# An attention and mixture-of-experts kernel: another opening, a later load of values, and half of a copy moved to VectorE in three steps

## The chip, the cores and the metric

The kernel runs on one core of one Trainium2 chip. The metric is the device time of one execution in microseconds (us). The engines are called as in the profile: PE is TensorE (PEld its weight loads), DVE is VectorE, ACT is ScalarE, POOL is GpSimd, SP is SyncE, which here only issues transfers. A time such as "at 8.08" is counted from the start of the profiled span.

## The reference

Attention over 4 batches, 8 heads, 768 positions and head dimension 64, with a window of 128 positions and 4 sink positions that all rows see; its output, as 3072 rows of 512, goes through a two-level top-1 mixture of experts (4 groups of 4 experts, hidden width 1024):

```python
scores = scale * np.matmul(q, k.transpose(0, 1, 3, 2))
is_sink = pos[None, :] < int(n_sink)
rel = pos[:, None] - pos[None, :]
in_window = (rel >= 0) & (rel < int(window))
scores = np.where(is_sink | in_window, scores, -1e9)
a = np.exp(scores - scores.max(-1, keepdims=True))
attn = np.matmul(a / (a.sum(-1, keepdims=True) + 1e-9), v)
...
g_idx = np.argmax(x @ w_group, axis=1)          # then the expert of the group in the same way
h = np.maximum(xg @ w1[g, e], 0.0)
out[tok_idx] = g_w * e_w * (h @ w2[g, e])
```

`n_sink` and `window` are inputs, so the masks are made on the chip from two 64-bit integers.

## The kernel before

**Tiling.** The 3072 rows are worked in 24 attention steps of 128 queries (6 per batch). The two halves of 64 queries of a step are folded onto 128 partitions, so that a head's scores are 128x136: 4 sink columns, 128 of the window, 4 more. The MoE follows in parts, and fills gaps of the later attention steps.

**One step.** In step i the code works on four ages of data: scores of i, transposes of a = i-1, values of b = i-2, and the router's logits of c = i-3. On PE, in the written order: `scores(i, 0)` and `scores(i, 1)` (four heads each, into two tiles `ps`, 32 products in all), `trans(a)` (16 transposes of the probabilities `pt` into `tp`), some products on zeros (`warm`, 8, 10 and 6 of them in steps 0 to 2, from the list `FILL`), `values(b, 0)`, `logits(c)`, `sink_t(a)` (two transposes of the sink probabilities `sp` into columns 256 to 319 of the same `tp`), `natural(c)` (transposes of the result), `values(b, 1)`. Where an age does not exist yet (steps 0 to 2) its part is missing.

On DVE: `maxima(i, g)` for the two halves g: one `COPY_PREDICATED` that folds the window's parts in `ps` (not in the first step of a batch), then for each of the four heads a masked copy `sm<-ps,msk` with the row's maximum. Then `norm(c)`, which scales the result (`xt<-tp,rc`), and in step 3 `tables()`, small tables for routing (`colm`, `trib` and others). On ACT: `evac(a, 0)` and `evac(a, 1)` copy the transposed probabilities of four heads each from `tp` in PSUM to `pa` in SBUF (two `COPY pa<-tp`); then the 8 exponentials of step i (`pt<-sm,st`), between them `sink_evac` (`spT`), and the copy of a result (`xT`). On POOL: for each half two selects (`pu<-pa`, `pa<-pa`) that split `pa`'s triangle, copies of the sink rows into `pu`, and the packing of `sp`.

**Buffers that tie them.** `sink_t(a)` writes columns of `tp` that the second half of `evac(a, ..)` reads (columns 256 to 511), so it waits for that copy. `scores(i+1)` writes the `ps` that `maxima(i)` reads. `values(b, 0)` and `(b, 1)` need `pa`, `pu` and the values `vv`.

**Order.** Each engine executes its instructions in the order in which the code records them; a wait of one holds all that stand behind it on that engine. The same holds for SP and its transfers. All instructions of these helpers carry line 118 in the profile, since one function records them.

**The opening.** POOL writes two integer tables (row minus column, and column). DVE casts them to `diff` and `col`, cuts `dq` out of `diff`, and makes the masks `msk`. The scalars come by a transfer `ni`, are cast to `nf` and spread to all partitions by one product with ones (`lg<-nf,colm`); DVE copies the result and rebuilds the two 64-bit numbers from their words in three instructions (`lneg` twice, `sv`; `sv` holds the sink count and the window), and a fourth makes `wd`. Before and after the product PE runs 14 and 6 products on zeros. `load_s(0)` and `load_v(0)`, the values of step 0, are issued ahead of the loop.

Of the kernel before, what the change touches and what calls it, by code (L numbers as in the profile page):

```python
# [22 lines left out]
P = 128  # L23
# [22 lines left out]
NEG = -1.0e30  # L46
# [101 lines left out]
def moe_attention(tc, kqT, vN, vS, nsw, wgx, wgd, w1, w2, out):  # L148
    nc = Pinned(tc)
    v = nc.vector  # L150
    with ExitStack() as top, ExitStack() as att:
# [17 lines left out]
        def const(shape, dt, name):  # L169
            return cp.tile(shape, dt, name=name)  # L170
# [10 lines left out]
        qb = wk.tile([P, NQ, HP, P], F32, name="qb", bufs=1)  # L181
        xx = un[:, 0:NDC * W].rearrange("p (c w) -> p c w", w=W)
        hx = un[:, NDC * W:(NDC + NFC) * W].rearrange("p (f w) -> p f w", w=W)
        dif = gp.tile([P, P], I32, name="xg")
        nc.gpsimd.iota(dif, pattern=[[-1, P]], base=0, channel_multiplier=1)
        coli = gp.tile([P, P], I32, name="xg")
        nc.gpsimd.iota(coli, pattern=[[1, P]], base=0, channel_multiplier=0)
        act = const([P, 1], F32, "act")
        nc.gpsimd.memset(act, 0.0)
        nc.gpsimd.memset(colm[0:1], 1.0)  # L190
        nc.gpsimd.memset(kb[:, :, 0:BW], 0.0)
        vts, env, bat = {}, {}, {}

# [71 lines left out]

        route_reset(tab)

        diff = const([P, P], F32, "diff")
        v.tensor_copy(diff, dif)
        col = const([P, P], F32, "col")  # L270
        v.tensor_copy(col, coli)
        dq = gp.tile([P, D], F32, name="xg")
        for r in (0, D):
            v.tensor_copy(dq[r:r + D], diff[r:r + D, r:r + D])
        isu = gp.tile([P, D], F32, name="xg")
        v.tensor_scalar(isu, dq, 0.0, None, ALU.is_lt)
        rel = gp.tile([P, D], F32, name="xg")
        v.scalar_tensor_tensor(rel, isu, float(P), dq, ALU.mult, ALU.add)
        nf1 = const([1, 4], F32, "nf1")
        v.tensor_copy(nf1, ni)  # L280
        warm(WARM)
        nc.tensor.matmul(ob[0][:, 0:4], colm[0:1], nf1, start=True, stop=True)
        warm(WARM2)
        msk = const([P, 3, SW], F32, "msk")
        mb, ms, mc = msk[:, :, 0:D], msk[:, :, D:D + 2 * NSK], msk[:, :, D + 2 * NSK:]
        v.tensor_scalar(mb[0:D, 0], dq[0:D], 0.0, NEG, ALU.mult, ALU.add)
        v.tensor_scalar(ms[:, 0, 0:NSK], col[:, 0:NSK], 0.0, NEG, ALU.is_ge, ALU.mult)
        wd = const([P, 1], F32, "wd")
        nf = const([P, 4], F32, "nf")
        v.tensor_copy(nf, ob[0][:, 0:4])  # L290
        lneg = const([P, 2], F32, "lneg")
        v.tensor_scalar(lneg, nf[:, 0::2], 0.0, 4294967296.0, ALU.is_lt, ALU.mult)
        v.tensor_tensor(lneg, lneg, nf[:, 0::2], ALU.add)
        sv = const([P, 2], F32, "sv")
        v.scalar_tensor_tensor(sv, nf[:, 1::2], 4294967296.0, lneg, ALU.mult, ALU.add)
        nsk, win = sv[:, 0:1], sv[:, 1:2]
        v.tensor_scalar(wd, win, -float(D), None, ALU.add)
        snk = gp.tile([P, D], F32, name="xg")
        v.tensor_scalar(mc[:, 2], rel, win, NEG, ALU.is_ge, ALU.mult)
        v.tensor_scalar(snk, col[:, 0:D], nsk, NEG, ALU.is_lt, ALU.mult)  # L300
        v.tensor_scalar(mb[:, 2], dq, wd, NEG, ALU.is_ge, ALU.mult)
        v.scalar_tensor_tensor(mc[:, 0], isu, NEG, mc[:, 2], ALU.mult, ALU.add)
        v.tensor_tensor(mb[D:P, 0], mb[D:P, 2], snk[D:P], ALU.add)
        v.tensor_scalar(ms[:, 0, NSK:], col[:, 0:NSK], nsk, NEG, ALU.is_ge, ALU.mult)
        v.tensor_tensor(mc[0:D, 0], mc[0:D, 0], snk[0:D], ALU.add)
        selu = const([P, D], I32, "selu")
        val = const([P, NI], F32, "val")

        def other_masks():
            v.tensor_scalar(selu, dq, 0.0, None, ALU.is_lt)  # L310
            v.tensor_copy(ms[:, 2], ms[:, 0])
            v.tensor_copy(msk[:, 1], msk[:, 2])
            v.tensor_tensor(snk[0:D], snk[0:D], isu[0:D], ALU.mult)
            v.tensor_tensor(mc[0:D, 1], mc[0:D, 1], snk[0:D], ALU.add)
# [19 lines left out]

        def tables():
            v.tensor_scalar(colm, col, -float(P), None, ALU.add)
            v.tensor_scalar(trib, diff, 0.0, None, ALU.is_lt)
            v.tensor_scalar(rev, col[:, 0:4], -1.0, 4.0, ALU.mult, ALU.add)
            v.tensor_scalar(edge, col[:, 0:MAXT + 1], float(P), None, ALU.mult)
            v.tensor_copy(val, prti)  # L340
            v.tensor_scalar(gen[:, 0:1], win, 1.0, None, ALU.is_lt)
            v.tensor_scalar(gen[:, 1:2], win, float(P), None, ALU.is_gt)
            v.tensor_scalar(gen[:, 2:3], nsk, float(NSK), None, ALU.is_gt)
            v.tensor_reduce(gen[:, 3:4], gen[:, 0:3], AX.X, ALU.max)
# [460 lines left out]
                    r = slice(f * D, (f + 1) * D)  # L805
                    nc.tensor.transpose(env["tp"][:, f, h * D:(h + 1) * D], e["pt"][r, h, NSK:NSK + P], ident[r, r])

        def evac(i, g):
            e = env[i]
            pa = wk.tile([P, 4, P], F32, name="pa", bufs=4)  # L810
            nc.scalar.copy(pa.rearrange("p h (f q) -> p f h q", f=2),
                           env["tp"][:, :, 4 * g * D:4 * (g + 1) * D].rearrange("p f (h q) -> p f h q", q=D))
            e["pT", g] = [pa, pu[i % 2][g]]
            if i % NT:
                for dst, sg in ((pu[i % 2][g], -1), (pa, 1)):
                    nc.gpsimd.affine_select(out=dst[0:D], in_=pa[0:D], pattern=[[0, 8], [sg, D]], compare_op=ALU.is_ge,
                                            fill=0.0, base=(sg - 1) // 2, channel_multiplier=-sg)
# [390 lines left out]

        ew = early_work(PARTS[0][0])
        room_v(-1)  # L1210
        load_s(0)
        load_v(0)
        rest = None
        for i in range(NI):
            a, b, c = i - 1, i - 2, i - 3
            mid, far, old = a >= 0, b >= 0, c >= 0
            state["clk"] += 3.0
            scores(i, 0)
            scores(i, 1)
            if i + DEPTH < NI:  # L1220
                load_q(i + DEPTH)
            if mid:
                env["tp"] = pair()
                trans(a)
                evac(a, 0)
                evac(a, 1)
            warm(FILL[i] if i < len(FILL) else 0, ob[0][:, 224:416])
            if far:
                values(b, 0)
                load_s(b + 1)  # L1230
            if i + DEPTH < NI:
                load_k(i + DEPTH)
            if i == 0:
                load_v(1)
            if old:
                logits(c)
            if mid:
                sink_t(a)
            if old:
                natural(c)  # L1240
            maxima(i, 0)
            exps(i, 0)
            maxima(i, 1)
            if i == NI - 1:
                sink_evac(a)
            if old:
                norm(c)
            routing(1, ("pe",))
            exps(i, 1, (0, 1))
            if mid and i < NI - 1:  # L1250
                sink_evac(a)
            exps(i, 1, (2, 3))
            if mid:
                sink_rows(a)
            if i < NI - 1:
# [396 lines left out]
```

## Time and profile before

| | us |
|---|---|
| median of 3 runs | 489.07 (487.38 to 489.42) |
| the profiled execution | 484.39 |
| its span, first to last instruction | 482.7 |
| outside the span | 1.69 |

The page of the profile gives, for each engine, its busy time over the span, and the chain of work that ended last, followed back from the last instruction. The timeline of one engine lists its instructions in order, neighbours of a kind in one row; a bracket gives the idle time ahead of a row and what released it. Spans of PE's rows overlap by about 0.07 us, since the ends of pipelined products are modelled. The name of a releaser is that of the semaphore event that came last, which need not be the one that mattered.

### The profile page before, as it was taken

How to read it: one execution, taken by the hardware profiler on the slowest of the kernel's cores; microseconds unless marked ns; L12 is line 12 of the kernel's file. 1: busy time of each engine (PE TensorE's matmuls, PEld its weight loads, DVE VectorE, ACT ScalarE, POOL GpSimd, SP SyncE). 2: the span in 40 equal slices, each digit the busy share in tenths (PEclk: the TensorE clock that was granted, in tenths of full speed). 3: DMA queues.
4: the chain of work that ended last, by engine and by line, in shares of the span. 5: the costliest groups of instructions: out<-in, count | busy, mean ns of one | idle time of the engine just before them, and what ended most of it. 6: DMA issues, size and time to landing. Idle time of an engine off the chain costs nothing.

```text
span 482.7 us, 14712 instructions
## 1 busy us (share of the span) xinstructions
PE 465.3 (96%) x5429; PEld 390.0 (81%) x5429; DVE 374.7 (78%) x1181; ACT 330.2 (68%) x858; POOL 168.4 (35%) x267
## 2 busy tenths in 40 slices
PE   7999999999989999999999999999999999999994
PEld 6788878888779888887989789569876977977974
DVE  7576888899989989987714876488687997999750
ACT  5999989899893445766615765278446786788741
POOL 3674765664662122221203124033302713103102
PEclk9999999999999999999999999999999999999998
DMA  8698878989978937934952358596949983999300
GB/s 260 177 286 277 275 250 245 272 258 318 289 233 274 336 103 245 311 135 150 377 217 85 110 176 299 197 330 267 311 169 372 411 314 111 362 405 337 108 22 30
DMA packets 58836, 117.09 MB, mean 243 GB/s; under 512 B 8574, under 2 KB 20990, under 8 KB 58754
## 3 DMA queue, kind: packets, MB, share of 16 engines
q1 hardware_dynamic: 54162, 102.65, 62.5%
q0 software_dynamic: 4320, 13.26, 7.8%
q8 instruction: 45, 0.74, 0.6%
q14 instruction: 37, 0.30, 0.2%
q10 hardware_dynamic: 272, 0.15, 0.1%
HBM read 103.25 MB, written 13.03 MB: 241 GB/s over the span
## 4 chain that ended last, share of the span: by engine, by line
PE 67%; DVE 17%; ACT 7%; issue 4%; POOL 3%; DMA 1%; POOLq 0%; DVEq 0%; SPq 0%; ACTq 0%
PE ph L118 30%; PE po L118 28%; PE tp L118 5%; ACT pt L118 3%; DVE sm L118 3%; DVE wlo L118 3%; PE ps L118 3%; DVE xt L118 2%; POOL pu L118 2%; ACT whi L118 1%; PE lg L118 1%; DVE ps L118 1%; ACT pa L118 1%; DVE lt L118 1%; DVE un L118 1%
## 5 line engine op out<-in xcount | busy, mean ns | idle before, releaser
L118 DVE TENSOR_TENSOR wlo<-rw,whi 128x1024 fp32r<-128x1024 f32 x112 | 135.0, 1223 | 24.9 <-ACT whi L118 23.5
L118 PE MATMUL ph<-un,whi 128*128 128x256 f32 (+9 forms) x576 | 128.0, 312 | 0.3
L118 PE MATMUL po<-whi,un 128*128 128x512 f32 (+5 forms) x384 | 127.8, 396 | 0.0
L118 ACT CAST whi<-rw 128x1024 fp32r<-128x1024 f32 (+1 forms) x115 | 115.6, 1025 | 10.5 <-DMA rw<-in_w 5.6
L118 POOL DMA_INDIRECT out<-ot,sidx x32 | 43.2, 1351 | 227.7 <-ACT ot L118 129.3
L118 PE MATMUL ph<-un,wlo 128*128 128x256 f32 (+10 forms) x416 | 99.1, 263 | 0.0
L118 PEld LDWEIGHTS ph<-un,whi 128*128 128x128 f32 x576 | 93.7, 189 | 2.2 <-DVE un L118 0.8
L118 PEld LDWEIGHTS po<-whi,un 128*128 128x128 f32 (+4 forms) x384 | 70.4, 185 | 25.1 <-issue 6.7
L118 ACT ACTIVATE pt<-sm,st 128x136 f32<-128x136 f32 x192 | 76.1, 402 | 7.4 <-DVE st L118 5.3
L118 PE MATMUL po<-wlo,un 128*128 128x512 f32 (+6 forms) x200 | 77.5, 389 | 0.0
L118 PEld LDWEIGHTS ph<-un,wlo 128*128 128x128 f32 x416 | 76.7, 189 | 0.6
L118 DVE CUSTOM_DVE_ANT_0 sm<-ps,msk 128x136 f32<-128x136 f32 x192 | 45.8, 296 | 7.3 <-PE ps L118 1.1
L118 PEld LDWEIGHTS po<-wlo,un 128*128 128x128 f32 (+5 forms) x200 | 36.0, 180 | 7.6
L118 POOL DMA_INDIRECT xg<-xd,gidx x30 | 33.1, 1104 | 24.2 <-DMA rw<-in_w 11.6
L118 PE MATMUL ps<-kb,qb 64*64 64x208 f32 (+1 forms) x768 | 38.4, 333 | 2.0 <-DVE st L118 1.4
L118 DVE TENSOR_TENSOR hc<-ph,hc 128x160 f32<-128x160 f32 (+6 forms) x64 | 21.3, 338 | 21.6 <-ACT hc L118 21.4
L118 POOL COPY pu<-spT 32x512 f32<-32x512 f32 x46 | 28.6, 649 | 26.3 <-ACT spT L118 25.4
L118 ACT ACTIVATION_READ_ACCUMULATOR pt<-sm,st 128x1 f32 x192 | 36.8, 192 | 0.0
L118 ACT ACTIVATE ot<-po,cg 128x512 f32<-128x512 f32 (+6 forms) x25 | 17.0, 681 | 28.1 <-PE po L118 28.1
L118 PEld LDWEIGHTS ps<-kb,qb 64*64 64x64 f32 x768 | 26.5, 132 | 7.3 <-DVE st L118 2.1
L118 POOL TENSOR_SCALAR_AFFINE_SELECT pu<-pa 64x512 f32<-64x512 f32 x40 | 26.4, 660 | 15.7 <-ACT pa L118 15.7
L118 ACT COPY hc<-ph 128x160 f32<-128x160 f32 (+6 forms) x64 | 19.4, 304 | 17.8 <-PE ph L118 17.0
(204 smaller groups left out, 717.6 us busy)
## 6 DMA issues: line engine op xcount, KB each, us to landing
rw<-in_w SPq DMA_DIRECT2D x128, 512.0 KB, 5.9
vv<-in_vN SPq DMA_DIRECT2D x24, 512.0 KB, 5.2
kb<-in_kqT SPq DMA_DIRECT2D x23, 288.0 KB, 3.9
qb<-in_kqT SPq DMA_DIRECT2D x24, 256.0 KB, 4.6
xd<-xt SPq DMA_DIRECT2D x24, 256.0 KB, 3.7
vv<-in_vS SPq DMA_DIRECT2D x24, 128.0 KB, 3.5
out<-ot,sidx POOLq DMA_INDIRECT x32, 4.9
xg<-xd,gidx POOLq DMA_INDIRECT x30, 4.9
```

Source lines behind the costliest of these rows:

```text
L118: r = f(*a, **k)
```

## The change

It has three parts.

1. **Opening.** POOL's IOTA writes `dq` (two blocks of 64x64) and `col` directly as f32; the casts and cuts on DVE are gone, and the table `diff` is made by a further IOTA in `tables()`, in step 3. The two scalars are combined on PE: `nf1` gets two more columns (is the low word negative), and three products with one row of ones or of 4294967296.0 add up in two columns of `lg`, each followed by one product on zeros (`WARM` 14 to 11, `WARM2` 6 to 1). The four instructions on DVE between the copy of the result and the masks are gone, and the masks that step 0 needs come from tables prepared earlier (`relx`, `far`). The table `rel` and the mask `mc[:, 2]` move into `other_masks()`, which runs after step 0's maxima.
2. **Values.** `load_s(0)` and `load_v(0)` are issued in step 0, after `load_k(2)`.
3. **Sharing.** In steps 1 to 3, `maxima(i, 0)` and `(i, 1)` are recorded ahead of `trans(a)` and `evac(a, ..)`, and the second half of `evac` is a copy by DVE; ACT keeps the first.

The core of the diff:

```diff
-        dif = gp.tile([P, P], I32, name="xg")
-        nc.gpsimd.iota(dif, pattern=[[-1, P]], base=0, channel_multiplier=1)
+        for r in (0, D):
+            count(dq[r:r + D], pattern=[[-1, D]], channel_multiplier=1)
+        count(col, pattern=[[1, P]], channel_multiplier=0)
...
-        nc.tensor.matmul(ob[0][:, 0:4], colm[0:1], nf1, start=True, stop=True)
-        warm(WARM2)
+        for k, (w, x) in enumerate(((colm[0:1], nf1[:, 0:4:2]), (two32, nf1[:, 4:6]), (two32, nf1[:, 1:4:2]))):
+            nc.tensor.matmul(ob[0][:, 0:2], w, x, start=k == 0, stop=k == 2)
+            warm(WARM2)
...
-        v.tensor_copy(nf, ob[0][:, 0:4])
-        v.tensor_scalar(lneg, nf[:, 0::2], 0.0, 4294967296.0, ALU.is_lt, ALU.mult)
-        v.tensor_tensor(lneg, lneg, nf[:, 0::2], ALU.add)
-        v.scalar_tensor_tensor(sv, nf[:, 1::2], 4294967296.0, lneg, ALU.mult, ALU.add)
+        v.tensor_copy(sv, ob[0][:, 0:2])
...
-        v.tensor_scalar(wd, win, -float(D), None, ALU.add)
+        v.tensor_scalar(mc[:, 0], relx, win, NEG, ALU.is_ge, ALU.mult)
+        v.tensor_scalar(mb[:, 2], far, win, NEG, ALU.is_ge, ALU.mult)
...
         def tables():
             v.tensor_scalar(colm, col, -float(P), None, ALU.add)
+            diff = gp.tile([P, P], F32, name="xg")
+            count(diff, pattern=[[-1, P]], channel_multiplier=1)
             v.tensor_scalar(trib, diff, 0.0, None, ALU.is_lt)
...
-        def evac(i, g):
+        def evac(i, g, copy=nc.scalar.copy):
...
-        load_s(0)
-        load_v(0)
...
+            early = mid and i <= SHARE
+            if early:
+                maxima(i, 0)
+                maxima(i, 1)
...
-                evac(a, 1)
+                evac(a, 1, v.tensor_copy if early else nc.scalar.copy)
...
             if i == 0:
+                load_s(0)
+                load_v(0)
                 load_v(1)
```

What stands in a row on three engines, before and after; in brackets the semaphores that a row waits for.

PE in the opening, around the product that spreads the scalars (`lg`; `tp<-wz` are the products on zeros), before:

```order
L118 LDWEIGHTS wz
L118 MATMUL tp<-wz 128x192
L118 MATMUL lg<-nf_145,colm 128x4 [waits DVE_49,Pool_49]
L118 LDWEIGHTS wz
L118 MATMUL tp<-wz 128x192 [waits PE_49]
```

Five more on zeros follow there before the first scores. The same place on PE after the change, up to the first scores (`xg` is the row of 4294967296.0):

```order
L119 MATMUL lg<-nf_140,colm 128x2 [waits DVE_49,Pool_49]
L119 LDWEIGHTS wz
L119 MATMUL tp<-wz 128x192 [waits PE_49]
L119 MATMUL lg<-nf_140,xg 128x2 [waits DVE_49,Pool_49]
L119 LDWEIGHTS wz
L119 MATMUL tp<-wz 128x192 [waits PE_49]
L119 MATMUL lg<-nf_140,xg 128x2
L119 LDWEIGHTS wz
L119 MATMUL tp<-wz 128x192 [waits PE_49]
L119 MATMUL ps_85<-kb,qb 64x136 [waits DMAHW2_49,DMAHW0_49,Pool_49]
```

One product `lg` with six on zeros behind it has become three with one behind each.

DVE from the last maxima of step 1 into step 2 (`ISA` are the masked copies with their maximum), before:

```order
L118 ISA sm,st<-ps_86,msk 128x136
L118 ISA st 128x1
L118 COPY_PREDICATED ps_85<-selu,ps_85 128x4x64 [waits PE_49]
L118 ISA sm,st<-ps_85,msk 128x136 [waits DVE_49,Activation_49]
L118 ISA st 128x1
```

Step 2's fold follows step 1's maxima at once. DVE at the same place after the change:

```order
L119 ISA sm,st<-ps_86,msk 128x136
L119 ISA st 128x1
L119 COPY pa<-tp 128x2x4x64 [waits Activation_49]
L119 COPY_PREDICATED ps_85<-selu,ps_85 128x4x64 [waits PE_49]
L119 ISA sm,st<-ps_85,msk 128x136 [waits DVE_49,Activation_49]
L119 ISA st 128x1
```

The copy of the second half of the transposed probabilities stands behind all eight maxima of the step, and waits for ACT's copy of the first half.

PE from `sink_t(0)` to `scores(2)`, before:

```order
L118 MATMUL tp<-ident,sp_120 96x64 [waits Activation_49,Pool_49]
L118 MATMUL tp<-ident,sp_120 96x64
L118 MATMUL ps_85<-kb,qb 64x208 [waits DMAHW1_49,DMAHW0_49,DVE_49]
L118 MATMUL ps_85<-kb,qb 64x208 x7
L118 MATMUL ps_86<-kb,qb 64x208 [waits DVE_49]
```

Here `sink_t` waits for ACT's copies, the scores for DVE's maxima. PE at the same place after the change:

```order
L119 MATMUL tp<-ident,sp_123 96x64 [waits DVE_49,Pool_49]
L119 MATMUL tp<-ident,sp_123 96x64
L119 MATMUL ps_85<-kb,qb 64x208 [waits DMAHW7_49,DMAHW6_49]
L119 MATMUL ps_85<-kb,qb 64x208 x7
L119 MATMUL ps_86<-kb,qb 64x208 x8
```

`sink_t` waits for DVE in place of ACT, and the scores behind it no longer wait for DVE themselves; the same holds for `sink_t(1)` and `sink_t(2)`. On SP the first eight transfers that follow `ni` are now queries, keys, queries, keys, queries, keys and then the two of values, where the values stood ahead of the third pair.

## Rows read from the trace of the kernel before

**Rows 1.** The page: busy time of each engine (share of the span), instructions.

```profile
PE 465.3 (96%) x5429; PEld 390.0 (81%) x5429; DVE 374.7 (78%) x1181; ACT 330.2 (68%) x858; POOL 168.4 (35%) x267
```

**Rows 2.** Busy time by engine in two stretches, granted clock, DMA share, rate.

```profile
0.00:15.08 15.08, 11.50 (x169) 9.10 (x170) 11.13 (x71) 9.30 (x37) 4.81 (x57) 1.00 0.77 241
15.08:138.00 122.92, 117.99 (x2983) 100.94 (x2984) 104.81 (x516) 113.03 (x432) 79.70 (x139) 1.00 0.88 269
```

**Rows 3.** PE's timeline, steps 0 to 4: start, us, operation, idle before.

```profile
1.13 2.42 PE L118 MATMUL tp<-wz 128*128 128x192 bf16 x14 [1.13 <-POOL wz L118]
3.48 0.59 PE L118 MATMUL lg<-nf,colm 1*128 1x4 f32 x2
...
8.08 1.64 PE L118 MATMUL ps<-kb,qb 64*64 64x208 f32 x32 [1.35 <-DVE st L118]
...
10.29 1.00 PE L118 MATMUL lg<-wz 128*128 128x192 bf16 x10
11.62 0.26 PE L118 MATMUL tp<-ident,sp 64*96 64x64 f32 x2 [0.33 <-ACT pa L118]
11.81 1.64 PE L118 MATMUL ps<-kb,qb 64*64 64x208 f32 x32
14.16 1.20 PE L118 MATMUL tp<-ident,pt 64*128 64x64 f32 x16 [0.71 <-ACT spT L118]
...
16.97 0.26 PE L118 MATMUL tp<-ident,sp 64*96 64x64 f32 x2
...
18.23 1.64 PE L118 MATMUL ps<-kb,qb 64*64 64x208 f32 x32
...
22.25 0.26 PE L118 MATMUL tp<-ident,sp 64*96 64x64 f32 x2
...
23.77 1.64 PE L118 MATMUL ps<-kb,qb 64*64 64x208 f32 x32
```

**Rows 4.** DVE's timeline in the opening and at the ends of maxima.

```profile
4.11 0.16 DVE L118 COPY nf<-lg 128x4 f32<-128x4 f32 x1 [0.62 <-PE lg L118]
...
6.45 0.30 DVE L118 CUSTOM_DVE_ANT_0 sm<-ps,msk 128x136 f32<-128x136 f32 x1 [0.16 <-DVE msk L118]
...
6.67 0.29 DVE L118 CUSTOM_DVE_ANT_0 sm<-ps,msk 128x136 f32<-128x136 f32 x1
...
9.07 0.43 DVE L118 COPY_PREDICATED ps<-selu,ps 128x256 f32<-128x256 int32 x1
...
12.12 0.08 DVE L118 DVE_READ_ACCUMULATOR2_ANT st<- 128x1 f32 x1
...
19.24 0.43 DVE L118 COPY_PREDICATED ps<-selu,ps 128x256 f32<-128x256 int32 x1 [2.83 <-PE ps L118]
...
22.14 0.08 DVE L118 DVE_READ_ACCUMULATOR2_ANT st<- 128x1 f32 x1
22.88 0.69 DVE L118 TENSOR_TENSOR xt<-tp,rc 128x512 f32<-128x512 f32 x1 [0.65 <-ACT pt L118]
...
23.91 0.21 DVE L118 TENSOR_SCALAR trib<-diff 128x128 bf16<-128x128 f32 x1
...
24.78 0.43 DVE L118 COPY_PREDICATED ps<-selu,ps 128x256 f32<-128x256 int32 x1
```

**Rows 5.** ACT's timeline: the copies of transposed probabilities.

```profile
10.40 1.07 ACT L118 COPY pa<-tp 128x512 f32<-128x512 f32 x2 [0.37 <-PE tp L118]
...
26.10 1.07 ACT L118 COPY pa<-tp 128x512 f32<-128x512 f32 x2 [0.31 <-PE tp L118]
```

**Rows 6.** POOL's timeline: the packing of step 3.

```profile
25.55 0.21 POOL L118 COPY sp<-pt 128x32 f32<-128x32 f32 x1
```

**Rows 7.** Transfers issued from 2 to 4 us: KB, us from issue to landing.

```profile
vv<-in_vN SPq DMA_DIRECT2D x1, 512.0 KB, 5.9
...
qb<-in_kqT SPq DMA_DIRECT2D x1, 256.0 KB, 4.4
...
vv<-in_vS SPq DMA_DIRECT2D x1, 128.0 KB, 5.2
```

More of the change, by code (lines that the diff above doesn't have):

```diff
@@ L65 @@
 HC = 3
+SHARE = 3
 LATE = 3
@@ L104 @@
 PW = G + NE
-WARM = 14
-WARM2 = 6
+WARM = 11
+WARM2 = 1
 FILL = [8, 10, 6]
@@ L183, in moe_attention, with count @@
         hx = un[:, NDC * W:(NDC + NFC) * W].rearrange("p (f w) -> p f w", w=W)
-        dif = gp.tile([P, P], I32, name="xg")
-        nc.gpsimd.iota(dif, pattern=[[-1, P]], base=0, channel_multiplier=1)
-        coli = gp.tile([P, P], I32, name="xg")
-        nc.gpsimd.iota(coli, pattern=[[1, P]], base=0, channel_multiplier=0)
+        mk = gp.tile([P, 6, D], F32, name="xg")
+        dq, far, isu, rel, relx, snk = (mk[:, k] for k in range(6))
+        col = const([P, P], F32, "col")
+        def count(out, **k):
+            nc.gpsimd.iota(out, base=0, allow_small_or_imprecise_dtypes=True, **k)
+        for r in (0, D):
+            count(dq[r:r + D], pattern=[[-1, D]], channel_multiplier=1)
+        count(col, pattern=[[1, P]], channel_multiplier=0)
         act = const([P, 1], F32, "act")
@@ L190, in moe_attention @@
         nc.gpsimd.memset(colm[0:1], 1.0)
+        two32 = gp.tile([1, P], F32, name="xg")
+        nc.gpsimd.memset(two32, 4294967296.0)
         nc.gpsimd.memset(kb[:, :, 0:BW], 0.0)
@@ L266, in moe_attention @@
         route_reset(tab)
[L268 to L275, printed above, removed]
-        v.tensor_scalar(isu, dq, 0.0, None, ALU.is_lt)
[L277 to L280, printed above, removed]
+        v.tensor_scalar(isu, dq, 0.0, None, ALU.is_lt)
+        v.scalar_tensor_tensor(relx, isu, -NEG, dq, ALU.mult, ALU.add)
+        v.tensor_scalar(far, dq, float(D), None, ALU.add)
+        nf1 = const([1, 6], F32, "nf1")
+        v.tensor_copy(nf1[:, 0:4], ni)
+        v.tensor_scalar(nf1[:, 4:6], nf1[:, 0:4:2], 0.0, None, ALU.is_lt)
         warm(WARM)
-        nc.tensor.matmul(ob[0][:, 0:4], colm[0:1], nf1, start=True, stop=True)
-        warm(WARM2)
+        for k, (w, x) in enumerate(((colm[0:1], nf1[:, 0:4:2]), (two32, nf1[:, 4:6]), (two32, nf1[:, 1:4:2]))):
+            nc.tensor.matmul(ob[0][:, 0:2], w, x, start=k == 0, stop=k == 2)
+            warm(WARM2)
         msk = const([P, 3, SW], F32, "msk")
@@ L287, in moe_attention @@
         v.tensor_scalar(ms[:, 0, 0:NSK], col[:, 0:NSK], 0.0, NEG, ALU.is_ge, ALU.mult)
-        wd = const([P, 1], F32, "wd")
-        nf = const([P, 4], F32, "nf")
-        v.tensor_copy(nf, ob[0][:, 0:4])
-        lneg = const([P, 2], F32, "lneg")
-        v.tensor_scalar(lneg, nf[:, 0::2], 0.0, 4294967296.0, ALU.is_lt, ALU.mult)
-        v.tensor_tensor(lneg, lneg, nf[:, 0::2], ALU.add)
         sv = const([P, 2], F32, "sv")
-        v.scalar_tensor_tensor(sv, nf[:, 1::2], 4294967296.0, lneg, ALU.mult, ALU.add)
+        v.tensor_copy(sv, ob[0][:, 0:2])
         nsk, win = sv[:, 0:1], sv[:, 1:2]
-        v.tensor_scalar(wd, win, -float(D), None, ALU.add)
-        snk = gp.tile([P, D], F32, name="xg")
-        v.tensor_scalar(mc[:, 2], rel, win, NEG, ALU.is_ge, ALU.mult)
         v.tensor_scalar(snk, col[:, 0:D], nsk, NEG, ALU.is_lt, ALU.mult)
-        v.tensor_scalar(mb[:, 2], dq, wd, NEG, ALU.is_ge, ALU.mult)
-        v.scalar_tensor_tensor(mc[:, 0], isu, NEG, mc[:, 2], ALU.mult, ALU.add)
-        v.tensor_tensor(mb[D:P, 0], mb[D:P, 2], snk[D:P], ALU.add)
+        v.tensor_scalar(mc[:, 0], relx, win, NEG, ALU.is_ge, ALU.mult)
+        v.tensor_scalar(mb[:, 2], far, win, NEG, ALU.is_ge, ALU.mult)
         v.tensor_scalar(ms[:, 0, NSK:], col[:, 0:NSK], nsk, NEG, ALU.is_ge, ALU.mult)
         v.tensor_tensor(mc[0:D, 0], mc[0:D, 0], snk[0:D], ALU.add)
+        v.tensor_tensor(mb[D:P, 0], mb[D:P, 2], snk[D:P], ALU.add)
         selu = const([P, D], I32, "selu")
@@ L309, in other_masks @@
         def other_masks():
+            v.scalar_tensor_tensor(rel, isu, float(P), dq, ALU.mult, ALU.add)
+            v.tensor_scalar(mc[:, 2], rel, win, NEG, ALU.is_ge, ALU.mult)
             v.tensor_scalar(selu, dq, 0.0, None, ALU.is_lt)
@@ L806, in trans @@
                     nc.tensor.transpose(env["tp"][:, f, h * D:(h + 1) * D], e["pt"][r, h, NSK:NSK + P], ident[r, r])
-        def evac(i, g):
+        def evac(i, g, copy=nc.scalar.copy):
             e = env[i]
             pa = wk.tile([P, 4, P], F32, name="pa", bufs=4)
-            nc.scalar.copy(pa.rearrange("p h (f q) -> p f h q", f=2),
-                           env["tp"][:, :, 4 * g * D:4 * (g + 1) * D].rearrange("p f (h q) -> p f h q", q=D))
+            copy(pa.rearrange("p h (f q) -> p f h q", f=2),
+                 env["tp"][:, :, 4 * g * D:4 * (g + 1) * D].rearrange("p f (h q) -> p f h q", q=D))
             e["pT", g] = [pa, pu[i % 2][g]]
@@ L1240, in moe_attention @@
                 natural(c)
-            maxima(i, 0)
+            if not early:
+                maxima(i, 0)
             exps(i, 0)
-            maxima(i, 1)
+            if not early:
+                maxima(i, 1)
             if i == NI - 1:
```

## The prediction

> **What bounds the kernel now.** I read the page's engine totals first, then the stretches, then each engine's timeline up to step 4. PE is busy for 96% of the span [rows 1]. The change touches only the opening and steps 1 to 3, so what matters is where PE stands still in there. In the first 15.08 us PE works 11.50; after that it works 117.99 of 122.92, DVE and ACT less [rows 2]. So what the change gains or loses before step 4 should go to the end one for one: from there PE hardly waits.
>
> PE's larger waits in there are 1.35 us ahead of `scores(1)`, 0.33 ahead of `sink_t(0)` and 0.71 inside step 2 [rows 3]. The reader should note two things. First, `sink_t` waits for the copy of transposed probabilities only once, for 0.33; at 16.97 and 22.25 it starts with no wait, as ACT's copies were ready long before. Second, DVE's maxima are late in a step: they fold `ps` 1.01 after the scores start (19.24 against 18.23; 24.78 against 23.77) and need 2.90 to the last read of a maximum (19.24 to 22.14) [rows 3, 4]. The maxima of a step thus end 3.91 after its scores start, the start of DVE's next instruction.
>
> The wait before `scores(1)` is named DVE, but its first half writes the `ps` that the fourth maximum leaves. Maxima start at 6.45 and come every 0.22 [rows 4], so the fourth ends at 6.45 + 3 x 0.22 + 0.30 = 7.41, and yet the scores start at 8.08. What is left is the transfer of keys 1. Its landing is not listed; the queries ahead of it in SP's row took 4.4 from their issue at 2.13, so 6.5, and the sink values behind it 5.2 from 3.11, so 8.3 [rows 7]. It landed between, and I take it for the releaser, at about 7.95.
>
> **The opening.** From the copy of the product at 4.11 to the first maximum at 6.45 DVE works off twelve small instructions, 2.34 / 12 = 0.20 each [rows 4]. Removed are the three that rebuild the numbers, `wd`, and one of seven masks: 5 x 0.20 = 1.0. Added on PE: two more products `lg`, and three on zeros in place of six; three fewer on zeros stand ahead. One `lg` is 0.59, of which the next row hides 0.07, so 0.52; the zeros at the start took 2.42 / 14 = 0.17 [rows 3]. Eleven of them end at 1.13 + 11 x 0.17 = 3.0; three `lg` and two zeros give 3 x 0.52 + 2 x 0.17 = 1.9, so the copy comes at 4.9 instead of 4.11. That takes 0.8 back of the 1.0. The scalars are ready sooner too, as DVE no longer casts two tables, but the zeros hide this. Net: the first maximum 0.2 earlier, bounds 0.1 later and 0.5 earlier.
>
> Nothing of it reaches PE, as `scores(1)` waits for keys 1. It would reach DVE's fold at 9.07, were it not for two small instructions (2 x 0.20) that now stand behind the maxima of step 0: 0.2 earlier, 0.4 later, and the fold can't run before 8.08 + 1.01 = 9.09 anyway. Term: fold 0.1 later (at 9.17), bounds 0.3 gained (keys 1 earlier) and 0.3 lost.
>
> **The values.** The transfer of values 0 (issue to landing 5.9 [rows 7]) moves behind queries 2 and keys 2. These wait for `scores(0)`, so values 0 are issued at about 7 and land at about 13. They are first needed by `values(0, 0)`, which stands right after the transposes and zeros of step 2, at about 16. Cover: 3 us. Keys 1 lose a neighbour and may land sooner, but then DVE holds the fold (above). Term: 0.
>
> **The sharing.** Here lies the sum. Of the two copies, ACT loses one: 1.07 less 0.01 over two is 0.53 [rows 5]. DVE gains one, which no row shows. Nearest is `xt<-tp,rc`, which also reads 128x512 f32 of PSUM: 0.69 [rows 4], and its successor starts about 0.60 after. From below I bound it by ACT's 0.53; from above by the fold's pace, 0.43 for 256 elements, so 0.86. I take 0.65, since the work is nearest to `xt`. PE sees the end of a copy 0.15 later (ACT's pair ends at 11.47, `sink_t(0)` starts at 11.62).
>
> But the copy now stands behind all the maxima of its step, and `sink_t` behind the copy, so `sink_t(a)` can start at scores(i) + 3.91 + 0.65 + 0.15 = scores(i) + 4.71, if PE is there. What stands behind it on PE is the rest of the step and the next scores, which the next maxima need: the delays add up.
>
> The Trainium skill ("VectorE: DVE Perf Modes", section "The perf-mode tier table") caps a copy from PSUM at twice the base rate, which by its cycle table would be an estimate of (120 + 256) / 0.96 = 0.39 us; its section "Why PSUM operands drop a tier" allows f32 only the base rate, an estimate of 0.66. By the first the sum below would be 3 x 0.26 = 0.8 less, a time of 490.0; no row here shows a plain copy from PSUM by VectorE, and `xt` has two operands, so the rows leave this open.
>
> - Step 1: the last maximum is read at 12.12 [rows 4], plus 0.1 for the fold; the copy ends at 12.87, `sink_t(0)` starts at 13.02 instead of 11.62. `scores(2)` follows after 0.19 (11.62 to 11.81), at 13.21 instead of 11.81: 1.40 late. Of this the 0.71 wait inside step 2 is won back, since ACT, 0.53 ahead, has the exponentials ready.
> - Step 2: `sink_t(1)` at 13.21 + 4.71 = 17.92. PE itself would be there at 13.21 + (16.97 - 11.81) - 0.71 less what else ACT held up there, so by 17.66 at the latest, and waits. `scores(3)` follows after 1.26 (16.97 to 18.23), at 19.18 instead of 18.23: 0.95 late.
> - Step 3: `sink_t(2)` at 19.18 + 4.71 = 23.89. PE is there after 22.25 - 18.23 = 4.02, at 23.2, and waits 0.7. `scores(4)` follows after 1.52 (22.25 to 23.77), at 25.41 instead of 23.77: **1.64 late**.
>
> From step 4 ACT makes both copies again, and finds in its row what it found before: at 26.10 it waited 0.31 for PE's transposes [rows 5]. So all is as before, 1.64 later.
>
> One edit reaches over this border. In step 3 DVE's `trib` waits for POOL's new IOTA, which stands behind the packing of step 3 (25.55 [rows 6]). POOL's selects of the second half, ahead of the packing, wait for DVE's copy, which ends at 19.18 + 3.91 + 0.65 = 23.7; by that I put the packing 1.0 to 1.3 later, at about 26.7, and with 0.2 each for it and the IOTA `trib` at about 27.1. From `trib` to the fold of step 4 it was 0.87 (23.91 to 24.78 [rows 4]), so the fold comes at 28.0 instead of 24.78 + 1.64 = 26.4. ACT's exponentials of step 4 start behind its copies, at 26.10 + 1.07 + 1.64 = 28.8 at the earliest, and the first maximum is there a fold and a maximum after 28.0 (0.43 + 0.30, and the gaps between), at 28.8 to 29.0. I take 0.1 on PE, bounds 0 and 0.3.
>
> Sum: 1.64, of which the opening is 0.1, plus 0 and 0.1: +1.7. On the profiled execution that is 484.39 + 1.7 = 486.1; the median lies 4.7 higher than that execution, and the same added to it gives **490.8**. Bounds: three copies at 0.53 or 0.86 are 0.36 less or 0.63 more; opening 0.4 less or 0.2 more; `trib` 0.1 less or 0.2 more. So +0.8 to +2.7, 489.9 to 491.8.
>
> **Rivals.** *The copy is hidden* (faster). If `sink_t` were not held by DVE, ACT's relief would count: the waits of 0.33 and 0.71 go, and 0.3 of the opening: 1.3 gained, 487.7. For it: ACT works 113.03 in 122.92 [rows 2], close to a bound, and loses 0.53 in each of three steps. Against it: the maxima's end at 3.91 after the scores, while PE comes to `sink_t` 4.0 to 4.5 after them and the copy with its 0.80 is still to be done.
>
> *TensorE slows down in the wider gap of step 1* (slower). All rows carry the full granted clock, 1.00 [rows 2], that is 2.4 GHz, yet the opening's zeros took 0.17 each and those of step 1 1.00 / 10 = 0.10 [rows 3], so the first ran at a lower pace, nearer to 1.2. With `sink_t(0)` at 13.02 PE stands still from 11.3 (10.29 + 1.00) for 1.7 us. If the pace drops there, `scores(2)` takes up to 1.6 more, all on the path: 490.8 + 1.6 = 492.4. Against it: after the 1.35 ahead of `scores(1)` the scores took 1.64, the same as at 11.81 [rows 3]; no row shows a standstill of 1.7 behind warm work. [...]
>
> *`trib` holds the fold longer* (slower). If the IOTA takes 1 us more than the packing before it, or POOL is that late, ACT waits that long in step 4, and PE's next values for ACT: 490.8 + 1.0 = 491.8 or more. It decides from a fold later than about 28.1, where ACT has done its copies.
>
> *Nothing moves.* If DVE's copy were to run between the maxima's halves, or waits were absorbed by later steps, 489.1. Against it: after 15.08 PE has only 4.9 us of idle time in 123 to absorb anything [rows 2], and that not on request.
>
> **How the numbers follow.** Forecast 0.72; copy hidden 0.07; lower pace 0.09; `trib` 0.06; nothing moves 0.06. The range has to hold 8 in 10: it takes in the forecast's own 489.9 to 491.8, the slower rivals up to 492.4, and below the case of no move and part of the first rival: 488.0 to 492.4. The bound for a change of 0.5%, about what a measurement of this kernel can tell from none, is 2.45 us: 486.6 and 491.5. Slower takes both slower rivals, 0.15, and a little of the forecast's upper end: 0.22. Faster needs nearly twice the gain of the first rival: 0.04. The rest is 0.74.
>
> **What would show it.** In the changed kernel's timeline: PE's wait ahead of `sink_t(0)` 1.7 instead of 0.33, and some 0.3 to 0.9 ahead of `sink_t(1)` and `sink_t(2)`, all released by DVE's copy; `scores(4)` at about 25.4; DVE's copies of 0.6 to 0.7; the fold of step 1 still at 9.1 to 9.2; the zeros and scores at their old durations. I am wrong if `scores(4)` starts at or before 23.8, if a copy on DVE takes under 0.4, or if PE's later steps swallow the delay.

## The result and the profile after

| | before | after |
|---|---|---|
| median us, 22 runs each | 487.47 (485.38 to 490.28) | 491.13 (486.83 to 495.6) |
| profiled execution, span | 484.39, 482.7 | 492.94, 491.1 |

The changed kernel is slower: the ratio is 1.006, 95% interval 1.0041 to 1.0078, that is +2.9 us (2.0 to 3.8). The ratio leaves out two executions of the changed kernel, 494.77 and 495.6, that fell into a slower state; the medians in the table hold them. The forecast was +1.7 (0.35%), below the 0.5% that the prediction took as what can be told from none; the measured change is 0.6%. That the forecast time of 490.8 lies near the measured 491.13 is luck: it was built on a median of three executions, 489.07, where 22 give 487.47, and +1.7 on that is 489.2.

The profiled pair lies 8.4 us apart, more than the medians. A part of that is not in the stretch that the change touches. Two stretches of the changed kernel (us, busy time of PE, PEld, DVE, ACT, POOL, granted clock, DMA share, GB/s):

```profile
0.00:15.08 15.08, 12.40 (x136) 9.60 (x140) 8.91 (x56) 8.05 (x33) 4.36 (x58) 1.00 0.70 210
104.00:130.00 26.00, 22.30 (x520) 19.14 (x514) 20.52 (x100) 21.40 (x82) 13.79 (x24) 0.93 0.90 276
```

Between 104 and 130 PE works 22.30 here and 24.38 before: this execution lost time there at a granted clock of 0.93 (before: 1.00) and in a wait of 2.13 us named "issue". The experiments below show "issue" waits of 0.2 to 1.8 at varying places between 55 and 131, in kernels with either opening, and in e1_opening and e2_share, one with each opening, the same clock of 0.93 in that stretch. From the start of `scores(9)` to the end of the span the thirteen profiles take 432.3 us (before) to 437.1 (after), and those between do not go by how late `scores(9)` start (e9_fewer_zeros, not late, 435.7; e3_opening_zeros, 2.5 late, 433.3). So I read these losses as belonging to the execution, which one profile of a kernel does not show, and take the start of each step's scores up to 60 us for what the change does.

One thing stays open in the time. Among the executions of the kernel before that were measured beside the experiments, a mean granted clock lower by 0.001 goes with 0.5 to 0.7 us more. They average 0.996 to 0.997, those of the changed kernel 0.995, so an estimated 1 us of the 2.9 may have come with the clock. Whether the change has a part in that is not shown; e6_no_zeros and e8_all_mended, which have its opening, average 0.997.

PE's timeline of the changed kernel, steps 0 to 6 (compare [rows 3]):

```profile
1.13 1.94 PE L119 MATMUL tp<-wz 128*128 128x192 bf16 x11 [1.13 <-POOL wz L119]
...
5.36 2.09 PE L119 MATMUL ps<-kb,qb 64*64 64x136 f32 x32
7.39 1.46 PE L119 MATMUL lg<-wz 128*128 128x192 bf16 x8
8.78 2.25 PE L119 MATMUL ps<-kb,qb 64*64 64x208 f32 x32
...
14.14 0.26 PE L119 MATMUL tp<-ident,sp 64*96 64x64 f32 x2 [1.54 <-DVE pa L119]
14.33 1.64 PE L119 MATMUL ps<-kb,qb 64*64 64x208 f32 x32
...
19.52 0.26 PE L119 MATMUL tp<-ident,sp 64*96 64x64 f32 x2 [1.22 <-DVE rc L119]
...
20.78 1.64 PE L119 MATMUL ps<-kb,qb 64*64 64x208 f32 x32
...
25.52 0.26 PE L119 MATMUL tp<-ident,sp 64*96 64x64 f32 x2 [0.93 <-DVE pa L119]
...
27.05 1.64 PE L119 MATMUL ps<-kb,qb 64*64 64x208 f32 x32
...
32.30 1.64 PE L119 MATMUL ps<-kb,qb 64*64 64x208 f32 x32
...
38.21 1.16 PE L119 MATMUL ps<-kb,qb 64*64 64x136 f32 x32
```

And of before, step 0 and the scores of steps 5 and 6:

```profile
4.81 1.16 PE L118 MATMUL ps<-kb,qb 64*64 64x136 f32 x32
5.90 0.83 PE L118 MATMUL lg<-wz 128*128 128x192 bf16 x8
...
29.04 1.64 PE L118 MATMUL ps<-kb,qb 64*64 64x208 f32 x32
...
34.48 1.16 PE L118 MATMUL ps<-kb,qb 64*64 64x136 f32 x32
```

Two things are to be seen. PE waits for DVE's copy ahead of each of the three `sink_t`, as forecast (the second is named `rc`, the instruction on DVE behind the copy). And, not forecast, the first scores take 2.09 and the zeros behind them 1.46 for eight, where before they took 1.16 and 0.83; the second scores take 2.25 instead of 1.64. Until about 10, PE works at little more than half its pace. By these lengths I take that for the lower of its two levels (1.2 against 2.4 GHz), though the granted clock in the row of the stretch is 1.00. `scores(4)` start at 27.05 instead of 23.77: 3.28 late, twice the forecast.

DVE's timeline of the changed kernel (compare [rows 4]):

```profile
10.40 0.43 DVE L119 COPY_PREDICATED ps<-selu,ps 128x256 f32<-128x256 int32 x1 [0.66 <-PE ps L119]
...
13.31 0.69 DVE L119 COPY pa<-tp 128x512 f32<-128x512 f32 x1
15.33 0.43 DVE L119 COPY_PREDICATED ps<-selu,ps 128x256 f32<-128x256 int32 x1 [1.34 <-PE ps L119]
16.35 0.30 DVE L119 CUSTOM_DVE_ANT_0 sm<-ps,msk 128x136 f32<-128x136 f32 x1 [0.59 <-ACT pt L119]
...
18.68 0.69 DVE L119 COPY pa<-tp 128x512 f32<-128x512 f32 x1
19.29 0.17 DVE L119 TENSOR_REDUCE rc<-sacc 128x16 f32<-128x32 f32 x1
...
28.85 0.23 DVE L119 TENSOR_SCALAR trib<-xg 128x128 bf16<-128x128 f32 x1 [1.95 <-POOL xg L119]
...
29.60 0.42 DVE L119 COPY_PREDICATED ps<-selu,ps 128x256 f32<-128x256 int32 x1
```

The fold of step 1 waits for PE and runs at 10.40 instead of 9.07. In step 2 the first maxima wait 0.59, by the profile's name for an exponential of step 1, whose buffer they write; before, only the second half of that step waited so, 0.37 at 15.06. The name explains little of it: that exponential ended at 15.85, PE's transposes, which wait for the same exponentials, start at 15.90, and the maxima only at 16.35. These maxima are the 64th DVE instruction of the trace, and at their 64th DVE instruction the six other profiles with the new opening have a pause of 0.19 to 0.20, named "issue". What held DVE there is open. `trib` waits 1.95 for the IOTA.

### The profile page after: what moved, and what is told of

The parts are those of the page before. It is cut to its first block, busy times and chain, and to the rows that moved or that the text cites. A ratio compares the mean times of both kernels' runs of the same rounds, so it can differ in the third digit from the quotient of the medians.

```text
span 491.1 us, 14703 instructions
## 1 busy us (share of the span) xinstructions
PE 469.9 (96%) x5427; PEld 393.0 (80%) x5427; DVE 374.5 (76%) x1179; ACT 328.7 (67%) x855; POOL 170.0 (35%) x270
## 4 chain that ended last, share of the span: by engine, by line
PE 67%; DVE 17%; ACT 6%; issue 4%; POOL 3%; DMA 1%; SPq 0%; POOLq 0%; DVEq 0%; ACTq 0%
PE ph L119 30%; PE po L119 28%; PE tp L119 5%; DVE sm L119 4%; PE ps L119 3%; DVE wlo L119 2%; ACT pt L119 2%; PE lg L119 2%; POOL pu L119 2%; DVE xt L119 2%; ACT whi L119 1%; DMA rw<-in_w 1%; DVE ps L119 1%; DVE un L119 1%; DVE lt L119 1%
## 5 line engine op out<-in xcount | busy, mean ns | idle before, releaser
L119 POOL DMA_INDIRECT out<-ot,sidx x32 | 44.5, 1391 | 227.9 <-ACT ot L119 130.0
L119 PE MATMUL ps<-kb,qb 64*64 64x208 f32 (+1 forms) x768 | 40.1, 344 | 2.9 <-issue 2.9
L119 POOL COPY pu<-spT 32x512 f32<-32x512 f32 x46 | 27.2, 617 | 27.7 <-ACT spT L119 26.4
L119 ACT COPY pa<-tp 128x512 f32<-128x512 f32 x45 | 24.4, 592 | 11.4 <-PE tp L119 11.3
```

What stands on the lines that cost most here:

```text
L119: r = f(*a, **k)
```

## The experiments

Theory after the trace: three costs. The sharing as forecast (1.64); a lower pace of PE in the new opening that delays step 1 (about 1.3); and `trib`, more than the 0.1 that I gave it. Rival: the sharing alone makes the 3 us, and the opening's delay is swallowed by the 0.71 that PE waited in step 2 before.

The starts on PE, read from each profile (us, one execution each; "8 zeros" are the products behind `scores(0)`; `scores(9)` are past all that the change touches):

| kernel | scores(0), took | 8 zeros took | scores(1), took | scores(4) | scores(9) |
|---|---|---|---|---|---|
| before | 4.81, 1.16 | 0.83 | 8.08, 1.64 | 23.77 | 50.40 |
| after | 5.36, 2.09 | 1.46 | 8.78, 2.25 | 27.05 | 53.98 |
| e1_opening | 5.50, 2.09 | 1.46 | 8.92, 1.68 | 24.65 | 51.99 |
| e2_share | 5.07, 1.76 | 0.83 | 8.32, 1.64 | 25.65 | 52.28 |
| e3_opening_zeros | 6.95, 1.85 | 0.83 | 9.49, 1.64 | 25.52 | 52.87 |
| e4_between | 5.07, 1.65 | 0.83 | 7.82, 1.64 | 23.05 | 49.72 |
| e5_iota_early | 5.50, 2.09 | 1.46 | 8.92, 2.04 | 25.01 | 51.62 |
| e6_no_zeros | 5.50, 2.09 | none | 7.91, 3.04 | 24.99 | 51.61 |
| e7_between_fill | 5.07, 1.42 | 0.83 | 8.26, 1.64 | 23.12 | 49.79 |
| e8_all_mended | 5.51, 2.09 | none | 7.81, 2.17 | 23.27 | 49.95 |
| e9_fewer_zeros | 4.22, 2.09 | 1.41 | 7.64, 1.64 | 23.73 | 50.34 |
| e10_three_together | 5.92, 2.09 | 1.01 | 8.88, 1.64 | 24.57 | 51.46 |
| e11_between5 | 4.97, 1.16 | 0.83 | 8.02, 1.64 | 23.06 | 49.90 |

**e1_opening**: the new opening alone.

```diff
-SHARE = 3
+SHARE = 0
...
+        load_s(0)
+        load_v(0)
         rest = None
...
-                load_s(0)
-                load_v(0)
                 load_v(1)
```

> The new opening alone: values 0 issued ahead of the loop and both copies on ACT as before. If the changed opening costs by its slower products (first theory), the zeros and scores of step 0 keep their long durations (scores(0) about 2.1 us, scores(1) about 2.2), the fold of step 1 runs at about 10.4, all behind it is 1.3 late, scores(4) start at about 25.1 and the time is 1.3 us above before. If the sharing alone makes the loss (rival), the opening's delay is swallowed by the 0.71 us that PE waits in step 2: scores(4) at about 24.3, time within 0.6 us of before.

Measured: ratio 1.0059 (1.0025 to 1.0092), +2.9 us (1.2 to 4.5). `scores(4)` at 24.65, 0.88 late: between the two expectations, as the higher pace came during `scores(1)` here. But the steps behind lose more. PE from step 0 to step 6, then what ACT, DVE and POOL do in steps 3 and 4:

```profile
5.50 2.09 PE L119 MATMUL ps<-kb,qb 64*64 64x136 f32 x32
7.53 1.46 PE L119 MATMUL lg<-wz 128*128 128x192 bf16 x8
8.92 1.68 PE L119 MATMUL ps<-kb,qb 64*64 64x208 f32 x32
...
29.91 1.66 PE L119 MATMUL ps<-kb,qb 64*64 64x208 f32 x32
31.59 1.19 PE L119 MATMUL tp<-ident,pt 64*128 64x64 f32 x16
33.16 1.15 PE L119 MATMUL po<-pa,vv 128*64 128x64 f32 x32 [0.38 <-POOL sp L119]
...
36.21 1.16 PE L119 MATMUL ps<-kb,qb 64*64 64x136 f32 x32
```

```profile
26.42 0.21 POOL L119 COPY sp<-pt 128x32 f32<-128x32 f32 x1
26.59 0.24 POOL L119 IOTA xg<- 128x128 f32 x1
...
26.86 0.23 DVE L119 TENSOR_SCALAR trib<-xg 128x128 bf16<-128x128 f32 x1 [1.98 <-POOL xg L119]
...
28.57 0.41 ACT L119 ACTIVATE pt<-sm,st 128x136 f32<-128x136 f32 x1 [0.53 <-DVE st L119]
```

The IOTA itself takes 0.24; that it stands behind the packing costs `trib` 1.98. The fold and maxima of step 4 come late, ACT waits 0.53, the transposes of step 5 take 1.19 instead of 0.71 since they wait for its exponentials, and `scores(5)` to `scores(6)` take 6.30 (29.91 to 36.21) where before they took 5.44 (29.04 to 34.48). The step after gives 0.14 back. At `scores(9)` 1.59 are left, within the interval of the time.

**e2_share**: the third part alone, on the kernel before.

```diff
+            early = mid and i <= SHARE
+            if early:
+                maxima(i, 0)
+                maxima(i, 1)
...
-                evac(a, 1)
+                evac(a, 1, v.tensor_copy if early else nc.scalar.copy)
```

> The sharing of steps 1 to 3 alone, with the opening and the values' order of before. First theory: sink_t(a) at scores(i) + 4.7, sink_t(0) at 12.95, no wait of the maxima of step 2 for ACT, scores(4) at about 25.4, time 1.6 us above before. Rival (the sharing makes all of it): scores(4) at about 27, time 3 us above before.

Measured: ratio 1.0025 (0.9992 to 1.0057), so the time alone does not tell it from no change. PE's timeline:

```profile
13.19 0.26 PE L119 MATMUL tp<-ident,sp 64*96 64x64 f32 x2 [1.65 <-DVE pa L119]
13.38 1.64 PE L119 MATMUL ps<-kb,qb 64*64 64x208 f32 x32
...
18.11 0.26 PE L119 MATMUL tp<-ident,sp 64*96 64x64 f32 x2 [0.78 <-DVE rc L119]
...
19.38 1.64 PE L119 MATMUL ps<-kb,qb 64*64 64x208 f32 x32
...
24.12 0.26 PE L119 MATMUL tp<-ident,sp 64*96 64x64 f32 x2 [0.93 <-DVE pa L119]
...
25.65 1.64 PE L119 MATMUL ps<-kb,qb 64*64 64x208 f32 x32
```

`sink_t(1)` stands 4.73 behind `scores(2)` and `sink_t(2)` 4.74 behind `scores(3)`; the forecast said 4.71. `scores(4)` are 1.88 late, of which 0.24 are the fold of step 1 (9.31 here, `scores(1)` at 8.32): 1.64 remain for the sharing. All of it is still there at `scores(9)`. The rival falls.

**e3_opening_zeros**: e1_opening with `WARM2 = 4` for 1.

> As e1_opening, with four products on zeros behind each of the three products in place of one. If the thin stretch of three small products between few zeros is what keeps PE at its lower pace, scores(0) now takes about 1.2 us and the zeros behind it 0.10 each, though the scalars come about 1 us later (copy of the scalars at about 6.4). If something else slows the products (the transfers, the keys), scores(0) stays at about 2.1 us.

Measured, one execution: the zeros behind `scores(0)` are back at 0.10 each, but most of `scores(0)` (1.85) still ran at the lower pace. So denser zeros help little: the higher pace comes at about 8.5 against about 9 in e1_opening, and the step is later by what the zeros take. The transfers do not explain the lower pace: from 5 to 10 us they run at 319 GB/s before, at 276 in e1_opening and at 155 after, and it is the last two that show the lower pace.

**e4_between**: e2_share with DVE's copy between the halves of the maxima.

```diff
             if early:
                 maxima(i, 0)
-                maxima(i, 1)
...
                 evac(a, 1, v.tensor_copy if early else nc.scalar.copy)
+            if early:
+                maxima(i, 1)
```

> As e2_share, with DVE's copy between the two halves of the maxima instead of behind both. If the place behind the maxima is what costs, the copy ends at scores(i) + 3.6, sink_t finds it ready, the waits of 0.33 and part of 0.71 us go, and scores(4) start at 23.0 to 23.5: time 0.3 to 0.8 us below before. If the copy's 0.65 us on DVE is what costs, wherever it stands, the second half of the maxima and the exponentials come late and scores(4) start at 24.3 or later.

Measured: ratio 0.9988 (0.9955 to 1.0022). PE's timeline:

```profile
11.86 0.27 PE L119 MATMUL tp<-ident,sp 64*96 64x64 f32 x2 [0.56 <-DVE pa L119]
12.05 1.98 PE L119 MATMUL ps<-kb,qb 64*64 64x208 f32 x32
...
16.48 0.26 PE L119 MATMUL tp<-ident,sp 64*96 64x64 f32 x2
...
17.75 1.64 PE L119 MATMUL ps<-kb,qb 64*64 64x208 f32 x32
...
23.05 1.64 PE L119 MATMUL ps<-kb,qb 64*64 64x208 f32 x32
```

The same copy, by the same engine, stands half a step's maxima earlier in its row, and starts 2.9 to 3.5 us behind the step's scores instead of 3.9 to 4.0 (now after a wait for ACT's copy of 0.40 to 0.93). PE waits no more ahead of `sink_t(1)` and `sink_t(2)`; 0.56 remain ahead of `sink_t(0)`, and `scores(2)` take 0.34 longer. `scores(4)` come 2.60 ahead of e2_share, of which 0.24 are the late `scores(1)` of e2_share, and 0.72 ahead of before; e11_between5, the same up to there, repeats that with 0.71. So the place behind the maxima is what costs, not the work on DVE. The gain against before is seen in the traces and not resolved in the time.

**e5_iota_early**: e1_opening with `diff` in a tile of its own, its IOTA at the end of the opening's list on POOL.

```diff
         route_reset(tab)
+        diff = const([P, P], F32, "diff")
+        count(diff, pattern=[[-1, P]], channel_multiplier=1)
...
-            diff = gp.tile([P, P], F32, name="xg")
-            count(diff, pattern=[[-1, P]], channel_multiplier=1)
```

> e1_opening with the IOTA of diff made by GpSimd in the opening instead of behind the packing of step 3. If that row's place is what costs in steps 4 and 5 (first theory), trib no longer waits 2 us, the fold of step 4 runs 1.0 us after the scores, scores(5) to scores(6) take 5.4 us as before instead of 6.3, and all from scores(6) on is 0.7 to 0.9 earlier than in e1_opening; scores(4) stay at about 24.7. If not, scores(5) to scores(6) stay at 6.3. Time against before: +0.9 (e1_opening by its trace +1.6).

Measured: ratio 1.0006 (0.9976 to 1.0037). PE's timeline:

```profile
30.27 1.64 PE L119 MATMUL ps<-kb,qb 64*64 64x208 f32 x32
31.84 0.71 PE L119 MATMUL tp<-ident,pt 64*128 64x64 f32 x16
...
35.71 1.16 PE L119 MATMUL ps<-kb,qb 64*64 64x136 f32 x32
```

From `scores(5)` to `scores(6)` it takes 5.44, as before: `trib` costs 0.86 there and 0.7 past it in e1_opening, and nothing here. The pace rose later in this profile (`scores(1)` 2.04), so `scores(4)` are 1.24 late.

**e6_no_zeros**: e5_iota_early with `FILL = [0, 10, 6]`.

> e5_iota_early without the 8 products on zeros behind scores(0). If it is these, at the lower pace, that keep PE busy until 8.9 and so delay scores(1), scores(1) now start when keys 1 have landed, at about 8.0, and scores(4) at about 23.9. If PE, with less work behind it, then runs scores(1) and the transposes at the lower pace too (2.2 us and more), the gain is lost: scores(4) at 24.5 or later.

Measured: ratio 0.9986 (0.9957 to 1.0015). PE's timeline:

```profile
7.91 3.04 PE L119 MATMUL ps<-kb,qb 64*64 64x208 f32 x32 [0.32 <-DMA kb<-in_kqT]
10.88 0.71 PE L119 MATMUL tp<-ident,pt 64*128 64x64 f32 x16
```

The second expectation held: the scores start when keys 1 are there, as forecast for the change, but all of them run at the lower pace and end where they ended with the zeros (10.95; 10.96 in e5_iota_early). Taking the zeros away wins nothing; the pace is what costs.

**e7_between_fill**: e4_between with `FILL = [8, 10, 0]`.

> e4_between without the 6 products on zeros of step 2. PE no longer waits for anything in step 2 there, so the zeros lie on the path: scores(4) 0.6 earlier, at about 22.4, and time 0.6 below e4_between, some 1.3 below before. If something else (ACT's copy, DVE's copy behind ACT's) is what ends last in step 2, scores(4) stay at 23.0.

Measured: ratio 0.9999 (0.997 to 1.0028), `scores(4)` at 23.12. A miss: where the zeros stood PE now waits, 0.42 for POOL's `pu` ahead of `sink_t(1)` (at 16.55).

**e8_all_mended**: the change with the copy between the maxima, the IOTA in the opening, values late, and `FILL = [0, 10, 0]`.

> The change with each cost taken out: DVE's copy between the halves of the maxima, the IOTA of diff in the opening, no zeros in steps 0 and 2; values late. If the three costs named are all there is, this is no slower than e7_between_fill within 0.5 us: scores(4) at 22.0 to 22.9, time 1.0 to 1.8 below before. If the new opening costs by itself (scalars 1.1 us later on DVE), scores(4) at 23.3 or later.

Measured: ratio 1.0002 (0.9972 to 1.0032), `scores(4)` at 23.27, 0.50 ahead of before but 0.22 behind e4_between. That is within 0.03 of the second expectation: the new opening still costs a little by itself (0.15 against e7_between_fill). The run also shows the second part of the change by itself:

```profile
7.81 2.17 PE L119 MATMUL ps<-kb,qb 64*64 64x208 f32 x32 [0.20 <-DVE st L119]
```

With the values issued late `scores(1)` no longer wait for keys 1 (in e6_no_zeros the row names them) but for DVE, and start 0.1 earlier. The later values neither cost nor bring more than that.

**e9_fewer_zeros**: the kernel before with `WARM = 11` and `WARM2 = 1`. **e10_three_together**: e5_iota_early with `WARM = 14`, the three products `lg` behind one another, then six zeros.

> The kernel before with only the numbers of zeros changed: 11 ahead of its one product lg and 1 behind, as in the change. If the number of products on zeros ahead of and behind the small products is what keeps PE at its lower pace, scores(0) now take about 2.1 us and scores(1) 1.7 or more, as with the new opening. If the three small products are the cause, scores(0) start at about 3.7, and PE reaches the higher pace no later than with the opening of before, by 6.7.

> e5_iota_early with the zeros of before around the three products: 14 ahead, the three directly behind one another, 6 behind. If the number of zeros is what counts, PE reaches the higher pace by about 6.7 as with the opening of before, and scores(1) take 1.64. If three small products in a row (1.6 us) are enough to hold the pace down, scores(0) take 2.1 and the zeros behind them 0.18 each, and the higher pace comes at 8.9 or later.

Measured, one execution each. PE of e9_fewer_zeros, then of e10_three_together:

```profile
4.22 2.09 PE L118 MATMUL ps<-kb,qb 64*64 64x136 f32 x32
6.25 1.41 PE L118 MATMUL lg<-wz 128*128 128x192 bf16 x8
7.64 1.64 PE L118 MATMUL ps<-kb,qb 64*64 64x208 f32 x32
```

```profile
5.92 2.09 PE L119 MATMUL ps<-kb,qb 64*64 64x136 f32 x32
7.95 1.01 PE L119 MATMUL lg<-wz 128*128 128x192 bf16 x8
8.88 1.64 PE L119 MATMUL ps<-kb,qb 64*64 64x208 f32 x32
```

Neither expectation holds alone. With fewer zeros and one product the higher pace comes at about 7.6, with three products and all zeros at about 8.2; with the opening of before it came at about 4.5 to 6.3 in five profiles (before, e2, e4, e7, e11), with the new one at about 8.5 to 10.9 in six (after, e1, e3, e5, e6, e8), as the lengths of single products show. Both the fewer zeros and the thin products seem to delay it; how much each has in it is not settled by one profile each. That e9_fewer_zeros loses nothing all the same (`scores(4)` at 23.73) shows when the pace matters: its `scores(0)` began 0.6 earlier, and the slow part was over at 7.64, ahead of the 8.08 at which `scores(1)` start before.

**e11_between5**: e4_between with `SHARE = 5`.

> e4_between with the sharing up to step 5 in place of 3. From step 4 PE hardly waits in e4_between (the first wait of more than 0.2 us comes at 36), so scores(4) stay at 23.1, scores(9) at 49.7 and the time at that of e4_between, 0.7 below before. If ACT still set the pace in steps 4 and 5, scores(6) come 0.3 or more earlier than 33.75.

Measured: ratio 0.9996 (0.9965 to 1.0028), `scores(6)` at 33.93. As expected, nothing is won behind step 3.

No version is shown to beat the kernel before; e4_between is ahead by 0.7 in the trace, which lies within the interval of its time.

## Why the prediction was right or wrong, point by point

- **Delays before step 4 go to the end**: right as far as the runs can tell. 3.28 at `scores(4)` and 3.58 at `scores(9)` in the trace, 2.9 (2.0 to 3.8) in the time.
- **The sharing, 1.64 with the opening's 0.1, so 1.54 by itself**: right in place, mechanism and size; measured 1.64. The rule scores(i) + 4.71 measured 4.73 and 4.74 (e2_share), and e4_between shows that it is the place in DVE's row. The copy's row is 0.69 long and its successor starts 0.61 later (18.68 to 19.29), against 0.65 taken. Of the two figures weighed from the Trainium skill ("VectorE: DVE Perf Modes"), the one by its section "Why PSUM operands drop a tier", 0.66, agrees; the copy came nowhere near the estimate of 0.39, to which the cap in "The perf-mode tier table" would let it go.
- **The opening, term 0.1**: wrong, the main miss. The step that failed is "nothing of it reaches PE, as `scores(1)` waits for keys 1". The scalars' copy came at 5.20 against 4.9 forecast: the zeros between the products took 0.27 each (3.52 to 3.79) instead of 0.17, and the 0.11 from the last product to the copy (4.00 to 4.11 before) was left out. The first maximum came at 6.64, 0.2 later than before and not 0.2 earlier. Above all PE did all of its opening at the lower pace, so that it was PE itself that was late for `scores(1)`: 0.70 at their start, 0.61 more in their length, fold at 10.40 instead of 9.17. I took the zeros' pace from a row and never asked what fewer zeros and more thin products would do to it; which of the two does it is not settled.
- **The step 2 term**: I had the maxima of step 2 free to run. They started 0.59 late, and `sink_t(1)` came at scores(2) + 5.19 instead of 4.71. The difference is not in e2_share (4.73), so it came with the opening and the sharing together, in the one profile that there is. The exponential that the profile names had ended 0.50 before; the cause stays open.
- **The slower rival** (lower pace) was the right resource in the wrong place: I put it into the gap of step 1. PE stood still there for 1.54 (after) and 1.65 (e2_share), and the scores behind took 1.64: that gap cost no pace.
- **`trib`, term 0.1, bounds 0 to 0.3**: mis-sized. Its time on DVE was right: the fold forecast 2.6 behind `scores(4)`, measured 2.55. The price on PE was 0.3 in the changed kernel (0.47 from `scores(5)` to `scores(6)`, 0.15 given back) and 0.7 in e1_opening, as the lateness runs on over ACT's wait into the transposes of step 5; I had followed it only to ACT's first exponential.
- **The values, term 0**: right. `values(0, 0)` start at 17.14 without a wait.
- **The time, 490.8**: near by luck, as said above.

The forecast's sum and the trace's: 1.64 of the sharing instead of 1.54; 1.64 more at `scores(4)` that came with the opening instead of 0.1; 0.3 of `trib` instead of 0.1. The second is 1.33 at the fold of step 1, less 0.14 since the maxima of step 1 run on without a gap (from the fold to `sink_t(0)` 3.74, in e2_share 3.88), and 0.46 of step 2 (5.19 against 4.73), to 0.01. That is +3.6 in one trace against +2.9 (2.0 to 3.8) in the time.

## What to carry to other kernels

Where a copy is handed to an engine that is less busy, look at what stands ahead of it in that engine's row when its result is due: here 0.65 us of work, placed behind the maxima, cost 1.6, and placed between them cost nothing. The products on zeros at a kernel's start are not only time on PE: here the opening with fewer of them and more thin products ran at the lower pace 2 to 6 us longer, so price such an opening at the lower pace up to the first wait that hides it. And a small table made later is not free because it is small: it comes when the engine that makes it gets there.

## What the runs showed that I had not expected

With the same opening, the profiles show PE's pace rise at different times: `scores(0)` took 1.16 (before, e11_between5), 1.42, 1.65 and 1.76 (e7, e4, e2), with the same products ahead on PE. The granted clock is 1.00 in these stretches, so that column doesn't show this; the length of equal products does: 0.18 and 0.10 each for the zeros.
